# A squared-ReLU MLP on one core: w2 in two loads, x ahead of w1 on two queues, and x's tail columns transposed in pairs of row tiles

## The chip, the cores and the metric

The kernel runs on one core of a Trainium2 chip. The metric is device time in microseconds. Twelve runs of the kernel before gave a median of 291.34 us, from 290.75 to 291.82.

The names used below: PE is TensorE, DVE is VectorE, ACT is ScalarE, POOL is GpSimd, SP is SyncE. SP computes nothing here; it issues DMAs. ACT and POOL can issue DMAs too. Each engine has its own list of instructions, and instructions of different engines are ordered by semaphores.

## The reference

Input x is 2048 x 576, w1 is 576 x 4608, w2 is 4608 x 576, all bf16, with two bias vectors.

```python
def reference(x, w1, b1, w2, b2):
    h = jnp.einsum("bsd,df->bsf", x, w1) + b1
    zero = jnp.zeros_like(h)
    r = jnp.where(h > zero, h, zero)
    h = r * r
    out = jnp.einsum("bsf,fd->bsd", h, w2) + b2
    return out
```

## The kernel before

**Tiling.** The 2048 rows of x are worked in four blocks of 512. The 4608 columns of w1 make 36 tiles of 128 (`ft`). The first four of these (`G`) have weights of their own, `w1n` (four row tiles of 128 by 512 columns) and `w1n8` (the last 64 rows of w1). The other 32 are worked in pairs: their weights `w1_h` hold one tile of the pair on partitions 0 to 63 and the other on 64 to 127, so that two matmuls of 64 rows run side by side (lines 188 and 190). For that, x transposed (`xT`, named xTw in the profile) is kept in nine slots of 64 or 128 rows, some of them copied to the other half of the partitions: `dup_windows` (lines 117 to 120) makes two copies of 64 x 2048 elements on DVE.

**Stages.** `a_full` computes the first four tiles of h for a block, `a_rows` the other 32. `evac_h` takes each tile out of PSUM: ACT applies the bias and ReLU (line 176), DVE squares (line 177). `phase_t` computes the last 128 output columns transposed (line 270, bias `b2T` added by ACT at line 273), `phase_b` the other 448 (line 289, bias `b2_bc` added by DVE at line 291). The blocks go in two pairs: a of blocks 0 and 1, then t and b of both, then the same for blocks 2 and 3.

**The start.** The first block's x is loaded as four row tiles `xs` (x_sb) and transposed on TensorE with an identity; the transposes of the later blocks are made by DMA (`load_xT`, lines 122 to 127). While the first x is awaited, seven matmuls on constants run (line 63). For the first block `a_full` runs in the order "k_outer": `x_transpose` (line 149) of row tiles 0 and 1, ten transposes; `x_copies(0)` (lines 151 to 159), which moves them from PSUM to xT0 with DVE and ACT; then partial matmuls `part(h, k)` (line 227) over halves h of the block's rows and row tiles k of w1n, with the transposes of row tiles 2 and 3 between them; then the `pair` matmuls over w1n8 (lines 203 and 205). For the last 64 columns of x, each row tile has a fifth transpose, of its last 128 columns. `make_b1T` transposes b1's 36 rows of 128.

**Queues.** SP's list of loads is x 0, w1n 0, w1n 1, x 3, w1n 2, w1n 3, then w1_h in pairs of halves with w1n8 behind the first pair, load_xT(1), the last four w1_h, b2_bc, six w2 loads of six row tiles each, load_xT(2). ACT loads x 1 and x 2. POOL loads b1_rows and b2_col (the last 128 values of b2, one to a partition) and then casts b2_col to b2T (line 102).

`keep(...)` holds an instruction at its place in the program's order. The pools `ps_h` and `ps_o` hold four PSUM banks each, handed out in turn; a tile that gets a bank again waits until its former reader is done.

Of the kernel before, what the change touches and what calls it, by code (L numbers as in the profile page):

```python
# [11 lines left out]
BF16 = mybir.dt.bfloat16  # L12
FP32 = mybir.dt.float32
# [4 lines left out]
def kernel(  # L18
# [9 lines left out]
    nc = tc.nc  # L28
    keep = tc.keep_in_program_order
    P = 128  # L30
    H = 64
    x2 = x.flatten_outer_dims()
    out2 = out.flatten_outer_dims()
    S, D = x2.shape
    F = w1.shape[1]
    NFT = F // P
    NC = D // H
    NK = NC // 2
    G = 4
    GW = G * P  # L40
# [4 lines left out]
    RT = SB // P  # L45
    DT = P
    DM = D - DT

    const = ctx.enter_context(tc.tile_pool(name="const", bufs=1))
    wpool = ctx.enter_context(tc.tile_pool(name="wpool", bufs=1))  # L50
# [5 lines left out]
    ps_h = ctx.enter_context(tc.tile_pool(name="ps_h", bufs=4, space=PSUM))  # L56
    ps_o = ctx.enter_context(tc.tile_pool(name="ps_o", bufs=4, space=PSUM))

    wps = ps_o.tile([P, 512], FP32, name="wps", tag="po")
    ones = nc.const_aps.tensor(1.0, [P, 512], BF16)  # L60
    WARM = [512] * 6 + [128]
    for i, n in enumerate(WARM):
        keep(nc.tensor.matmul(wps[:, 0:n], lhsT=ones[:, 0:P], rhs=ones[:, 0:n], start=True, stop=True))  # L63

    xs = const.tile([P, RT, D], BF16, name="x_sb")
    w1n = wpool.tile([P, NK, GW], BF16, name="w1n")
    w1n8 = wpool.tile([P, G // 2, P], BF16, name="w1n8")
    w1_h = wpool.tile([P, NC, FH], BF16, name="w1_h")
    w1_v = w1.rearrange("(c p) f -> p c f", p=H)

    def load_x(eng, rt):
        keep(eng.dma_start(out=xs[:, rt, :], in_=x2[rt * P:(rt + 1) * P, :]))  # L72

    def load_w1n(eng, k):
        keep(eng.dma_start(out=w1n[:, k, :], in_=w1[k * P:(k + 1) * P, 0:GW]))  # L75

    def load_w1n8(eng, h):
        src = w1[NK * P:D, 0:GW].rearrange("p (i h f) -> p i h f", h=2, f=P)
        keep(eng.dma_start(out=w1n8[h * H:(h + 1) * H, :, :], in_=src[:, :, h, :]))

    def load_w1(eng, h, j0, j1):
        keep(eng.dma_start(out=w1_h[h * H:(h + 1) * H, :, j0 * P:j1 * P],
                      in_=w1_v[:, :, GW + h * FH + j0 * P:GW + h * FH + j1 * P]))

    load_x(nc.sync, 0)
    load_x(nc.scalar, 1)
    load_w1n(nc.sync, 0)
    load_x(nc.scalar, 2)
    load_w1n(nc.sync, 1)
    load_x(nc.sync, 3)  # L90
    for k in range(2, NK):
        load_w1n(nc.sync, k)

    ident = const.tile([P, P], BF16, name="ident")
    make_identity(nc, ident[:])
    b1_rows = const.tile([P, P], BF16, name="b1_rows")
    nc.gpsimd.memset(b1_rows[:], 0.0)
    nc.gpsimd.dma_start(out=b1_rows[0:NFT, :], in_=b1.rearrange("(ft p) -> ft p", p=P))
    b2_col = const.tile([P, 1], BF16, name="b2_col")
    nc.gpsimd.dma_start(out=b2_col[:], in_=b2[DM:D].rearrange("(d o) -> d o", o=1))  # L100
    b2T = const.tile([P, 1], FP32, name="b2T")
    nc.gpsimd.tensor_copy(out=b2T[:], in_=b2_col[:])
    warm = const.tile([P, 1], FP32, name="warm")
    keep(nc.scalar.activation(out=warm[:], in_=nc.const_aps.tensor(0.0, [P, 1], FP32), func=ACT.Relu))

    E3, O, SPC, E = 0, 1, 5, 6
    LO_W = [O, O + 1, O + 2, O + 3, E, E + 1, E + 2, E3, SPC]
# [9 lines left out]
    def dup_windows(sb):  # L117
        xT = xT_blk[sb]
        keep(nc.vector.tensor_copy(out=xT[0:H, SPC:SPC + 4, :], in_=xT[H:P, E3:E3 + 4, :]))  # L119
        keep(nc.vector.tensor_copy(out=xT[H:P, SPC:SPC + 4, :], in_=xT[0:H, O:O + 4, :]))  # L120
# [7 lines left out]

    w2_sb = wpool.tile([P, NFT, D], BF16, name="w2_sb")
    w2_view = w2.rearrange("(ft p) d -> p ft d", p=P)  # L130
    W2CH = 6

    def load_w2(c):
        keep(nc.sync.dma_start(out=w2_sb[:, c * W2CH:(c + 1) * W2CH, :], in_=w2_view[:, c * W2CH:(c + 1) * W2CH, :]))
# [3 lines left out]
    alloc_xT(0)  # L138
    xT0 = xT_blk[0]
    HS = SB // 2  # L140
    tb_po = [ps_o.tile([P, 2, HS], BF16, name="tb", tag="po") for _ in range(2)]
    tb_ph = [ps_h.tile([P, 2, HS], BF16, name="tb", tag="ph") for _ in range(4)]
    half_banks = [tb_ph, None]

    def x_transpose(j, k):
        h, q = divmod(j, 2)
        qc = slice(q * P, (q + 1) * P)
        bank, slot, c0 = (half_banks[h][k], 0, k * P) if k < NK else (half_banks[h][2], 1, D - P)
        keep(nc.tensor.transpose(bank[:, slot, qc], xs[:, j, c0:c0 + P], ident[:]))  # L149

    def x_copies(h):
        hc = slice(h * HS, (h + 1) * HS)
        for k in range(NK):
            src = half_banks[h][k][:, 0, :]
            if k % 2 == 0:
                keep(nc.vector.tensor_copy(out=xT0[:, O + k, hc], in_=src))  # L156
            else:
                keep(nc.scalar.copy(out=xT0[:, O + k, hc], in_=src))  # L158
        keep(nc.vector.tensor_copy(out=xT0[:, E3, hc], in_=half_banks[h][2][:, 1, :]))


    b1T = const.tile([P, NFT], FP32, name="b1T")

    def make_b1T():
        b1T_ps = ps_o.tile([P, P], BF16, name="b1T_ps", tag="po")
        keep(nc.tensor.transpose(b1T_ps[:], b1_rows[:], ident[:]))  # L166
        keep(nc.vector.tensor_copy(out=b1T[:], in_=b1T_ps[:, 0:NFT]))

# [26 lines left out]
    def a_full(sb, order):  # L195
        xT = xT_blk[sb]
        banks = []
        for g in range(G):
            pool, tag = (ps_o, "po") if g < 2 else (ps_h, "ph")
            banks.append(pool.tile([P, SB], FP32, name="pn", tag=tag))  # L200

        def pair(i, start, stop):
            keep(nc.tensor.matmul(banks[2 * i][:], lhsT=w1n8[0:H, i, :], rhs=xT[0:H, SPC, :],  # L203
                             start=start, stop=stop, skip_group_check=order == "k_outer"))
            keep(nc.tensor.matmul(banks[2 * i + 1][:], lhsT=w1n8[H:P, i, :], rhs=xT[H:P, E3, :],  # L205
                             start=start, stop=stop, skip_group_check=order == "k_outer"))

        def full(g, k, start, stop):
            keep(nc.tensor.matmul(banks[g][:], lhsT=w1n[:, k, g * P:(g + 1) * P], rhs=xT[:, O + k, :],  # L209
                             start=start, stop=stop))  # L210

        if order == "rows_first":
            for i in (1, 0):
                pair(i, True, False)
            for g in (2, 3, 0, 1):
                for k in range(NK):
                    full(g, k, False, k == NK - 1)
                evac_h(sb, banks[g], g)
        else:
            if order == "k_outer":  # L220
                tb_new = [ps_h.tile([P, 2, HS], BF16, name="tb", tag="ph") for _ in range(2)]
                half_banks[1] = tb_new + tb_po

                def part(h, k):
                    hc = slice(h * HS, (h + 1) * HS)
                    for g in range(G):
                        keep(nc.tensor.matmul(banks[g][:, hc], lhsT=w1n[:, k, g * P:(g + 1) * P],  # L227
                                              rhs=xT[:, O + k, hc], start=(h == 0 and k == 0), stop=False,
                                              skip_group_check=True))

                for j in range(2):
                    for k in range(NK):
                        x_transpose(j, k)
                for j in range(2):
                    x_transpose(j, NK)
                x_copies(0)
                part(0, 0)
                for k in range(NK + 1):
                    x_transpose(2, k)
                part(0, 1)  # L240
                part(0, 2)
                for k in range(NK + 1):
                    x_transpose(3, k)
                x_copies(1)
                dup_windows(0)
                part(0, 3)
                part(1, 0)
                make_b1T()
                for k in range(1, NK):
                    part(1, k)  # L250
            else:
                for g in (2, 3, 0, 1):
                    for k in range(NK):
                        full(g, k, k == 0, False)
            for i in (1, 0):
                pair(i, False, True)
                evac_h(sb, banks[2 * i], 2 * i)
                evac_h(sb, banks[2 * i + 1], 2 * i + 1)
# [35 lines left out]
    for (j0, j1) in [(0, 1), (1, 2), (2, 4), (4, 6), (6, 8), (8, 10), (10, 12)]:  # L294
        load_w1(nc.sync, 0, j0, j1)
        load_w1(nc.sync, 1, j0, j1)
        if j0 == 0:
            load_w1n8(nc.sync, 0)
            load_w1n8(nc.sync, 1)
    load_xT(1)  # L300
    for (j0, j1) in [(12, 14), (14, 16)]:
        load_w1(nc.sync, 0, j0, j1)
        load_w1(nc.sync, 1, j0, j1)
    keep(nc.sync.dma_start(out=b2_bc[:], in_=b2.partition_broadcast(P)))
    for c in (0, 3, 1, 4, 2, 5):
        load_w2(c)
    load_xT(2)

# [51 lines left out]
```

## Time and profile before

One execution was taken by the hardware profiler. Beside the lines shown in the prediction, these are the values to have at hand:

| what | value |
|---|---|
| median of 12 runs | 291.34 us |
| profiled execution, own time | 291.82 us |
| its span, first to last instruction | 290.1 us |
| granted TensorE clock | 1.0 |
| first x transpose on PE starts | 3.39 us |
| PE idle from 6.36 to 6.95 us, for a w1n transfer | 0.59 us |
| first pair of `a_rows` on PE starts | 10.45 us |
| first read of w2 on PE starts | 76.6 us |
| last w2 load issued, and its time to landing | 36.65 us, 10.5 us |

A time that the text calls a start is counted from the start of the span. A line of the timeline gives start, duration, engine with source line, operation, the tile written and the tile read, and how often. In brackets stands how long the engine was idle before, and what ended that. An engine's name with a q (SPq) is its instruction queue, issuing DMAs. Busy shares of different engines overlap, so they do not add up to the span.

### The profile page before, as it was taken

How to read it: one execution, taken by the hardware profiler on the slowest of the kernel's cores; microseconds unless marked ns; L12 is line 12 of the kernel's file. 1: busy time of each engine (PE TensorE's matmuls, PEld its weight loads, DVE VectorE, ACT ScalarE, POOL GpSimd, SP SyncE). 2: the span in 40 equal slices, each digit the busy share in tenths (PEclk: the TensorE clock that was granted, in tenths of full speed). 3: DMA queues.
4: the chain of work that ended last, by engine and by line, in shares of the span. 5: the costliest groups of instructions: out<-in, count | busy, mean ns of one | idle time of the engine just before them, and what ended most of it. 6: DMA issues, size and time to landing. Idle time of an engine off the chain costs nothing.

```text
span 290.1 us, 4699 instructions
## 1 busy us (share of the span) xinstructions
PE 285.7 (98%) x2032; PEld 139.7 (48%) x2032; DVE 78.5 (27%) x176; ACT 96.6 (33%) x154; POOL 2.2 (1%) x10
## 2 busy tenths in 40 slices
PE   8999999999999999999999999999999999999995
PEld 4644444444444555555544444444444455555554
DVE  1644554444500200000015444444440001100001
ACT  2566666666500000000027666666670000000000
POOL 3000000000000000000000000000000000000000
DMA  7999999300001200000000000000000110000000
GB/s 200 215 244 192 313 390 220 76 0 2 0 13 26 52 16 18 16 16 18 16 16 2 1 2 0 2 0 2 0 2 0 36 38 16 16 17 30 21 16 18
DMA packets 31637, 16.52 MB, mean 57 GB/s; under 512 B 15732, under 2 KB 31616, under 8 KB 31616
## 3 DMA queue, kind: packets, MB, share of 16 engines
q1 hardware_dynamic: 31264, 15.91, 21.9%
q8 instruction: 16, 0.26, 0.4%
q10 hardware_dynamic: 288, 0.30, 0.3%
q14 instruction: 5, 0.04, 0.0%
q0 software_dynamic: 64, 0.01, 0.0%
HBM read 11.36 MB, written 2.36 MB: 47 GB/s over the span
## 4 chain that ended last, share of the span: by engine, by line
PE 97%; DMA 1%; SPq 1%; issue 0%; DVE 0%
PE ph L188 42%; PE po L289 38%; PE pt L270 11%; PE pn L209 4%; DMA w1n<-in_w_dram 1%; PE pn L227 1%; PE ph L190 1%; PE pn L203 1%; SPq L75 0%; SPq L72 0%; DVE o_sb L291 0%; PE tb L149 0%; PE b1T_ps L166 0%; PE pn L205 0%
## 5 line engine op out<-in xcount | busy, mean ns | idle before, releaser
L188 PE MATMUL ph<-xTw,w_h 64*128 64x512 bf16 x576 | 124.6, 376 | 0.0
L190 PE MATMUL ph<-xTw,w_h 64*128 64x512 bf16 x576 | 124.6, 376 | 0.0
L289 PE MATMUL po<-w_sb,hT 128*128 128x448 bf16 (+2 forms) x612 | 109.4, 341 | 0.0
L176 ACT ACTIVATE r<-ph,b1T 128x512 bf16<-128x512 f32 x128 | 81.0, 684 | 41.7 <-PE ph L190 41.7
L188 PEld LDWEIGHTS <-w_h 64*128 64x128 bf16 x576 | 54.1, 94 | 68.3
L289 PEld LDWEIGHTS <-hT 128*128 128x128 bf16 x612 | 58.5, 98 | 51.0
L177 DVE TENSOR_TENSOR hT<-r 128x512 bf16<-128x512 bf16 x144 | 61.1, 425 | 75.9 <-ACT r L176 75.4
L190 PEld LDWEIGHTS <-w_h 64*128 64x128 bf16 x576 | 54.1, 94 | 0.0
L291 DVE TENSOR_TENSOR o_sb<-po,b_bc 128x448 bf16<-128x448 f32 (+2 forms) x17 | 10.1, 597 | 125.8 <-PE po L289 125.8
L270 PE MATMUL pt<-hT,w_sb 128*128 128x512 bf16 x144 | 31.4, 379 | 0.0
L176 ACT ACTIVATE r<-pn,b1T 128x512 bf16<-128x512 f32 x16 | 10.3, 687 | 61.0 <-PE pn L205 59.6
L270 PEld LDWEIGHTS <-w_sb 128*128 128x128 bf16 x144 | 14.1, 98 | 17.0
L273 ACT ACTIVATE oT<-pt,b2T 128x512 bf16<-128x512 f32 x4 | 2.7, 687 | 28.3 <-PE pt L270 28.3
L209 PE MATMUL pn<-xTw,w1n 128*128 128x512 bf16 x48 | 10.9, 379 | 0.0
L209 PEld LDWEIGHTS <-w1n 128*128 128x128 bf16 x48 | 4.5, 98 | 6.0 <-issue 0.8
L227 PE MATMUL pn<-xTw,w1n 128*128 128x256 bf16 x32 | 4.6, 289 | 0.6 <-DMA w1n<-in_w_dram 0.6
L227 PEld LDWEIGHTS <-w1n 128*128 128x128 bf16 x32 | 3.1, 103 | 1.2 <-DMA w1n<-in_w_dram 0.9
L63 PE MATMUL wps<-const-bfloat16-1.0 128*128 128x512 bf16 (+1 forms) x7 | 2.8, 578 | 0.8 <-PEq L344 0.8
L156 DVE COPY xTw<-tb 128x256 bf16<-128x256 bf16 x4 | 1.1, 292 | 6.9 <-PE tb L149 6.9
L119 DVE COPY xTw<-xTw 64x2048 bf16<-64x2048 bf16 x4 | 2.8, 690 | 0.2
L120 DVE COPY xTw<-xTw 64x2048 bf16<-64x2048 bf16 x4 | 2.8, 688 | 0.1
L158 ACT COPY xTw<-tb 128x256 bf16<-128x256 bf16 x4 | 1.3, 375 | 3.9 <-PE tb L149 3.9
(23 smaller groups left out, 16.2 us busy)
## 6 DMA issues: line engine op xcount, KB each, us to landing
w_sb<-in_w_dram SPq DMA_DIRECT2D x6, 864.0 KB, 9.8
w_h<-in_w_dram SPq DMA_DIRECT2D x14, 288.0 KB, 6.4
out_dram<-o_sb SPq DMA_DIRECT2D x15, 112.0 KB, 1.7
w_h<-in_w_dram SPq DMA_DIRECT2D x4, 144.0 KB, 3.4
w1n<-in_w_dram SPq DMA_DIRECT2D x4, 128.0 KB, 4.0
out_dram<-ot SPq DMA_DIRECT2D x4, 128.0 KB, 2.0
x_sb<-in_x_dram ACTq DMA_DIRECT2D x2, 144.0 KB, 3.0
x_sb<-in_x_dram SPq DMA_DIRECT2D x2, 144.0 KB, 3.2
```

Of the source, the lines that this page charges most:

```text
L63: keep(nc.tensor.matmul(wps[:, 0:n], lhsT=ones[:, 0:P], rhs=ones[:, 0:n], start=True, stop=True))
L119: keep(nc.vector.tensor_copy(out=xT[0:H, SPC:SPC + 4, :], in_=xT[H:P, E3:E3 + 4, :]))
L176: keep(nc.scalar.activation(out=r[:], in_=bank[:], func=ACT.Relu, bias=b1T[:, ft:ft + 1], scale=1.0))
L177: keep(nc.vector.tensor_tensor(out=hTs[sb][:, ft, :], in0=r[:], in1=r[:], op=ALU.mult))
L188: keep(nc.tensor.matmul(bx[:], lhsT=w1_h[0:H, LO_C[i], jc], rhs=xT[0:H, LO_W[i], :], start=(i == 0), stop=(i == NC - 1)))
L190: keep(nc.tensor.matmul(by[:], lhsT=w1_h[H:P, UP_C[i], jc], rhs=xT[H:P, UP_W[i], :], start=(i == 0), stop=(i == NC - 1)))
L203: keep(nc.tensor.matmul(banks[2 * i][:], lhsT=w1n8[0:H, i, :], rhs=xT[0:H, SPC, :], start=start, stop=stop, skip_group_check=order == "k_o ...
L209: keep(nc.tensor.matmul(banks[g][:], lhsT=w1n[:, k, g * P:(g + 1) * P], rhs=xT[:, O + k, :], start=start, stop=stop))
L227: keep(nc.tensor.matmul(banks[g][:, hc], lhsT=w1n[:, k, g * P:(g + 1) * P], rhs=xT[:, O + k, hc], start=(h == 0 and k == 0), stop=False, s ...
L270: keep(nc.tensor.matmul(pt[:], lhsT=w2_sb[:, ft, DM:D], rhs=hT[:, ft, :], start=(i == 0), stop=(i == NFT - 1)))
L289: keep(nc.tensor.matmul(po[:, 0:d1 - d0], lhsT=hT[:, ft, jj * P:(jj + 1) * P], rhs=w2_sb[:, ft, d0:d1], start=(i == 0), stop=(i == NFT - 1)))
L291: keep(nc.vector.tensor_tensor(out=o_sb[:, d0:d1], in0=po[:, 0:d1 - d0], in1=b2_bc[:, d0:d1], op=ALU.add))
```

## The change

- x comes first: row tiles 0 and 2 on SP, 1 and 3 on ACT. The four w1n loads follow, alternately on SP and ACT. The two w1n8 loads, now each of all 512 columns, and the b1 load are issued by ACT, after its table load. The zeroing of b1_rows goes from POOL to DVE.
- b2_col is loaded by SP, after the last w1_h load and before b2_bc. The cast to b2T stays on POOL; in the program it now stands behind the w1_h loads and before the call of `a_full`.
- w2 is loaded in two transfers of 18 row tiles each instead of six of six.
- `x_transpose(j)` makes the four full transposes of a row tile. The 64 tail columns of two row tiles are put side by side in `xs8` by a copy on POOL and transposed together, so there are 16 + 2 = 18 transposes instead of 20. DVE copies the result to two slots of xT0, and three more copies on DVE fill the duplicate slots, in place of `dup_windows(0)`.
- All transposes and copies of the first block now stand before the first `part`.
- The line 63 matmuls write to a bank of ps_h instead of ps_o, and the last has 256 columns instead of 128; the four banks of the first `a_full` all come from ps_o, the transposes and b1T_ps from ps_h.

```diff
-    wps = ps_o.tile([P, 512], FP32, name="wps", tag="po")
+    wps = ps_h.tile([P, 512], FP32, name="wps", tag="ph")
-    WARM = [512] * 6 + [128]
+    WARM = [512] * 6 + [256]
...
+    b1_rows = const.tile([P, P], BF16, name="b1_rows")
+    nc.vector.memset(b1_rows[:], 0.0)
     load_x(nc.sync, 0)
     load_x(nc.scalar, 1)
-    load_w1n(nc.sync, 0)
-    load_x(nc.scalar, 2)
-    load_w1n(nc.sync, 1)
-    load_x(nc.sync, 3)
-    for k in range(2, NK):
-        load_w1n(nc.sync, k)
+    load_x(nc.sync, 2)
+    load_x(nc.scalar, 3)
+    for k in range(NK):
+        load_w1n(nc.sync if k % 2 == 0 else nc.scalar, k, k + 1)
 
     ident = const.tile([P, P], BF16, name="ident")
     make_identity(nc, ident[:])
-    b1_rows = const.tile([P, P], BF16, name="b1_rows")
-    nc.gpsimd.memset(b1_rows[:], 0.0)
-    nc.gpsimd.dma_start(out=b1_rows[0:NFT, :], in_=b1.rearrange("(ft p) -> ft p", p=P))
-    b2_col = const.tile([P, 1], BF16, name="b2_col")
-    nc.gpsimd.dma_start(out=b2_col[:], in_=b2[DM:D].rearrange("(d o) -> d o", o=1))
-    b2T = const.tile([P, 1], FP32, name="b2T")
-    nc.gpsimd.tensor_copy(out=b2T[:], in_=b2_col[:])
     warm = const.tile([P, 1], FP32, name="warm")
     keep(nc.scalar.activation(out=warm[:], in_=nc.const_aps.tensor(0.0, [P, 1], FP32), func=ACT.Relu))
+    for h in range(2):
+        load_w1n8(nc.scalar, h)
+    keep(nc.scalar.dma_start(out=b1_rows[0:NFT, :], in_=b1.rearrange("(ft p) -> ft p", p=P)))
...
-    W2CH = 6
+    W2CH = 18
...
+    def x_transpose(j):
         h, q = divmod(j, 2)
-        qc = slice(q * P, (q + 1) * P)
-        bank, slot, c0 = (half_banks[h][k], 0, k * P) if k < NK else (half_banks[h][2], 1, D - P)
-        keep(nc.tensor.transpose(bank[:, slot, qc], xs[:, j, c0:c0 + P], ident[:]))
+        for k in range(NK):
+            bank, slot = PLACE[k]
+            keep(nc.tensor.transpose(tb[h][bank][:, slot, q * P:(q + 1) * P], xs[:, j, k * P:(k + 1) * P], ident[:]))
+
+    def x_transpose_tail(h):
+        keep(nc.gpsimd.tensor_copy(out=xs8[:, 2 * h:2 * h + 2, :], in_=xs[:, 2 * h:2 * h + 2, NK * P:D]))
+        keep(nc.tensor.transpose(tb[1][0][:, 2, h * P:(h + 1) * P], xs8[:, 2 * h:2 * h + 2, :], ident[:]))
+
+    def x_copies_tail():
+        src = tb[1][0][:, 2, :].rearrange("p (h t) -> p h t", h=2)
+        for q in range(2):
+            keep(nc.vector.tensor_copy(out=xT0_q[H:P, E3, :, q, :], in_=src[q * H:(q + 1) * H, :, :]))
+        for q in range(2):
+            keep(nc.vector.tensor_copy(out=xT0_q[0:H, SPC, :, q, :], in_=src[q * H:(q + 1) * H, :, :]))
+        keep(nc.vector.tensor_copy(out=xT0[0:H, E:E + 3, :], in_=xT0[H:P, O:O + 3, :]))
+        keep(nc.vector.tensor_copy(out=xT0[0:H, E3, :], in_=xT0[H:P, O + 3, :]))
+        keep(nc.vector.tensor_copy(out=xT0[H:P, SPC:SPC + 4, :], in_=xT0[0:H, O:O + 4, :]))
 
     def x_copies(h):
         hc = slice(h * HS, (h + 1) * HS)
-        for k in range(NK):
-            src = half_banks[h][k][:, 0, :]
-            if k % 2 == 0:
-                keep(nc.vector.tensor_copy(out=xT0[:, O + k, hc], in_=src))
-            else:
-                keep(nc.scalar.copy(out=xT0[:, O + k, hc], in_=src))
-        keep(nc.vector.tensor_copy(out=xT0[:, E3, hc], in_=half_banks[h][2][:, 1, :]))
+        for k in (0, 1):
+            keep(nc.vector.tensor_copy(out=xT0[:, O + k, hc], in_=tb[h][0][:, k, :]))
+        keep(nc.scalar.copy(out=xT0[:, O + 2:O + 4, hc], in_=tb[h][1][:, 0:2, :]))
...
                 for j in range(2):
-                    for k in range(NK):
-                        x_transpose(j, k)
-                for j in range(2):
-                    x_transpose(j, NK)
+                    x_transpose(j)
                 x_copies(0)
-                part(0, 0)
-                for k in range(NK + 1):
-                    x_transpose(2, k)
-                part(0, 1)
-                part(0, 2)
-                for k in range(NK + 1):
-                    x_transpose(3, k)
+                for j in range(2, RT):
+                    x_transpose(j)
                 x_copies(1)
-                dup_windows(0)
-                part(0, 3)
+                for h in range(2):
+                    x_transpose_tail(h)
+                x_copies_tail()
+                for k in range(NK):
+                    part(0, k)
                 part(1, 0)
                 make_b1T()
...
         load_w1(nc.sync, 1, j0, j1)
-        if j0 == 0:
-            load_w1n8(nc.sync, 0)
-            load_w1n8(nc.sync, 1)
     load_xT(1)
     for (j0, j1) in [(12, 14), (14, 16)]:
         load_w1(nc.sync, 0, j0, j1)
         load_w1(nc.sync, 1, j0, j1)
+    b2_col = const.tile([P, 1], BF16, name="b2_col")
+    keep(nc.sync.dma_start(out=b2_col[:], in_=b2[DM:D].rearrange("(d o) -> d o", o=1)))
+    b2T = const.tile([P, 1], FP32, name="b2T")
+    nc.gpsimd.tensor_copy(out=b2T[:], in_=b2_col[:])
     keep(nc.sync.dma_start(out=b2_bc[:], in_=b2.partition_broadcast(P)))
-    for c in (0, 3, 1, 4, 2, 5):
+    for c in range(2):
         load_w2(c)
     load_xT(2)
```

More of the change, by code (lines that the diff above doesn't have):

```diff
@@ L66 @@
     w1n = wpool.tile([P, NK, GW], BF16, name="w1n")
-    w1n8 = wpool.tile([P, G // 2, P], BF16, name="w1n8")
+    w1n8 = wpool.tile([P, GW], BF16, name="w1n8")
     w1_h = wpool.tile([P, NC, FH], BF16, name="w1_h")
@@ L72, in load_x, with load_w1n @@
         keep(eng.dma_start(out=xs[:, rt, :], in_=x2[rt * P:(rt + 1) * P, :]))
-    def load_w1n(eng, k):
-        keep(eng.dma_start(out=w1n[:, k, :], in_=w1[k * P:(k + 1) * P, 0:GW]))
+    def load_w1n(eng, k0, k1):
+        src = w1[k0 * P:k1 * P, 0:GW].rearrange("(k p) f -> p k f", p=P)
+        keep(eng.dma_start(out=w1n[:, k0:k1, :], in_=src))
     def load_w1n8(eng, h):
-        src = w1[NK * P:D, 0:GW].rearrange("p (i h f) -> p i h f", h=2, f=P)
-        keep(eng.dma_start(out=w1n8[h * H:(h + 1) * H, :, :], in_=src[:, :, h, :]))
+        keep(eng.dma_start(out=w1n8[h * H:(h + 1) * H, :], in_=w1[NK * P:D, 0:GW]))
     def load_w1(eng, h, j0, j1):
@@ L140 @@
     HS = SB // 2
[L141 to L145, printed above, removed]
-        h, q = divmod(j, 2)
-        qc = slice(q * P, (q + 1) * P)
-        bank, slot, c0 = (half_banks[h][k], 0, k * P) if k < NK else (half_banks[h][2], 1, D - P)
-        keep(nc.tensor.transpose(bank[:, slot, qc], xs[:, j, c0:c0 + P], ident[:]))
+    tb = [[ps_h.tile([P, 4, HS], BF16, name="tb", tag="ph") for _ in range(2)] for _ in range(2)]
@@ new lines @@
+    PLACE = [(0, 0), (0, 1), (1, 0), (1, 1)]
+    xs8 = const.tile([P, RT, H], BF16, name="xs8")
+    xT0_q = xT0.rearrange("p c (h q t) -> p c h q t", h=2, q=2)
+    def x_transpose(j):
+        h, q = divmod(j, 2)
+        for k in range(NK):
[4 more added lines that the diff above has]
+        keep(nc.tensor.transpose(tb[1][0][:, 2, h * P:(h + 1) * P], xs8[:, 2 * h:2 * h + 2, :], ident[:]))
@@ L162 @@
+        keep(nc.scalar.copy(out=xT0[:, O + 2:O + 4, hc], in_=tb[h][1][:, 0:2, :]))
     b1T = const.tile([P, NFT], FP32, name="b1T")
     def make_b1T():
-        b1T_ps = ps_o.tile([P, P], BF16, name="b1T_ps", tag="po")
+        b1T_ps = ps_h.tile([P, P], BF16, name="b1T_ps", tag="ph")
         keep(nc.tensor.transpose(b1T_ps[:], b1_rows[:], ident[:]))
@@ L198, in a_full @@
         for g in range(G):
-            pool, tag = (ps_o, "po") if g < 2 else (ps_h, "ph")
+            pool, tag = (ps_o, "po") if g < 2 or order == "k_outer" else (ps_h, "ph")
             banks.append(pool.tile([P, SB], FP32, name="pn", tag=tag))
         def pair(i, start, stop):
-            keep(nc.tensor.matmul(banks[2 * i][:], lhsT=w1n8[0:H, i, :], rhs=xT[0:H, SPC, :],
+            keep(nc.tensor.matmul(banks[2 * i][:], lhsT=w1n8[0:H, 2 * i * P:(2 * i + 1) * P], rhs=xT[0:H, SPC, :],
                              start=start, stop=stop, skip_group_check=order == "k_outer"))
-            keep(nc.tensor.matmul(banks[2 * i + 1][:], lhsT=w1n8[H:P, i, :], rhs=xT[H:P, E3, :],
+            keep(nc.tensor.matmul(banks[2 * i + 1][:], lhsT=w1n8[H:P, (2 * i + 1) * P:(2 * i + 2) * P], rhs=xT[H:P, E3, :],
                              start=start, stop=stop, skip_group_check=order == "k_outer"))
@@ L220, in a_full @@
             if order == "k_outer":
-                tb_new = [ps_h.tile([P, 2, HS], BF16, name="tb", tag="ph") for _ in range(2)]
-                half_banks[1] = tb_new + tb_po
                 def part(h, k):
```

## The prediction

> **What bounds the kernel now.** I read the page's busy shares first, then the chain that ended last, then the timelines of PE, SP and POOL over the first 35 us, since the diff touches little beyond the start.
>
> ```profile
> PE 285.7 (98%) x2032; PEld 139.7 (48%) x2032; DVE 78.5 (27%) x176; ACT 96.6 (33%) x154; POOL 2.2 (1%) x10
> ...
> PE ph L188 42%; PE po L289 38%; PE pt L270 11%; PE pn L209 4%; DMA w1n<-in_w_dram 1%; PE pn L227 1%; PE ph L190 1%; PE pn L203 1%; SPq L75 0%; SPq L72 0%; DVE o_sb L291 0%; PE tb L149 0%; PE b1T_ps L166 0%; PE pn L205 0%
> ```
>
> TensorE is busy for 98% of the span and carries 97% of the chain. So there is almost nothing to win: before the end, only the DMA pieces of 1% are not matmuls. The other side is that TensorE has no slack behind which a new wait could disappear. A wait put in front of the first matmuls moves everything after it.
>
> The PE timeline at the start (start, duration, instruction; in brackets the idle time and what ended it):
>
> ```profile
> 0.78 2.82 PE L63 MATMUL wps<-const-bfloat16-1.0 128*128 128x512 bf16 x7 [0.78 <-PEq L344]
> ...
> 3.39 1.27 PE L149 MATMUL tb<-ident,x_sb 128*128 128x128 bf16 x10
> ...
> 6.95 0.61 PE L227 MATMUL pn<-xTw,w1n 128*128 128x256 bf16 x4 [0.59 <-DMA w1n<-in_w_dram]
> ...
> 8.60 1.47 PE L227 MATMUL pn<-xTw,w1n 128*128 128x256 bf16 x12
> 10.01 0.39 PE L203 MATMUL pn<-xTw,w1n 64*128 64x512 bf16 x1
> ```
>
> The first pair over w1's last 64 rows starts at 10.01; this is my reference point, because after it both programs issue the same matmuls in the same order. Before it the one stall of note is 0.59 us (with 0.87 on the weight loads) for a w1n transfer.
>
> Then SP's and POOL's own timelines:
>
> ```profile
> 6.36 12.04 SPq L82 DMA_DIRECT2D w_h<-in_w_dram  x12
> 18.45 4.60 SPq L126 DMA_TRANSPOSE xTw<-in_x_dram  x1
> 23.10 1.25 SPq L127 DMA_TRANSPOSE xTw<-in_x_dram  x1
> 24.39 2.65 SPq L82 DMA_DIRECT2D w_h<-in_w_dram  x4
> 27.09 0.67 SPq L304 DMA_DIRECT2D b_bc<-in_b_dram  x1
> ...
> 2.12 0.56 POOL L100 DMA_DIRECT2D b_col<-in_b_dram  x1
> 5.89 0.18 POOL L102 CAST b2T<-b_col 128x1 f32<-128x1 bf16 x1 [3.21 <-DMA b_col<-in_b_dram]
> ```
>
> SP issues all of w1 and two transposes before it reaches b2_bc at 27.09. POOL waits 3.21 us for b2_col and then casts it. Today this harms nobody, since nothing stands behind the cast on POOL. Last, what the DMA view (size and time from issue to landing) says of issues near 26 to 27 us:
>
> ```profile
> w_h<-in_w_dram SPq DMA_DIRECT2D x2, 288.0 KB, 6.7
> ...
> b_bc<-in_b_dram SPq DMA_DIRECT2D x1, 144.0 KB, 6.4
> ```
>
> **What the Trainium skill says.** "TensorE: Matmul & The Clock Gate", table at the head of the page: the queues of ScalarE, VectorE and GpSimdE are strict FIFO. No run here shows it for POOL yet (its cast is last), but the step below rests on it. The same page, Part 1: after an idle window of about 3.4 us the array falls back to half rate, and about 3.4 us of sustained work restore it. The trace agrees with a slow start: the 512-column weight loads of L63 start 0.43 us apart, the matmuls of L188 0.215 us apart. L227's matmuls take 417 ns at most and 273 in the median. "DMA: Bandwidth & Descriptors", Queues, rings and completion order: each engine consumes a ring's descriptors in order; here b2_bc, issued at 27.09, lands at 33.5, behind w1's last 288 KB (about 26.4 plus 6.7, 33.1).
>
> **The change part by part.**
>
> *b2_col and the cast (the term that decides).* The load moves from POOL's queue at 2.12 to SP's, behind all of w1 and load_xT(1), at the place of b2_bc. The cast of b2T stays on POOL, and in the program it stands before a_full, so before the two new copies into xs8. The compiled order of the changed kernel confirms it:
>
> ```
> POOL  L302 TensorCopy b2T<-b_col 128x1      [waits the b2_col DMA]
> POOL  L149 TensorCopy xs_121<-x_sb 128x128  [waits x 0, x 1]
> POOL  L149 TensorCopy xs_121<-x_sb 128x128  [waits x 2, x 3]
> PE    L150 Ldweights xs_121                 [waits POOL]
> PE    L230 Ldweights w1n                    (the first of the 32 partial matmuls)
> ```
>
> So the tail transposes, and behind them on PE every matmul of w1n, wait for a DMA of 256 bytes at the end of SP's list. When does it land? SP's early list loses two w1n (0.90 us) and two w1n8 issues (1.30) to ACT, but in the compiled order each later issue waits for the DMA eight places earlier, so SP starts w1 at about 3.6 as now (x 1 was issued at 0.73 and lands 2.8 later). By my walk through these waits the first 288 KB go out near 6.5 instead of 7.7, 1.2 us sooner. From 10 us on the DMA share of the windows is near or over 1.0, so the lead can only be kept. Landing L is then 33.1 - 1.2 plus some 0.2 for its own descriptors: 32.1 us. Bounds: 30 (lead of the full 2.2 us, landing 5 after issue at 25) and 33.5 (no lead, landing where b2_bc does).
>
> After L: cast 0.18 plus 0.07 to wake (5.89 against 2.12 + 3.7 for the landing). Two POOL copies of 128x128 are not in the trace; nearest are POOL's MEMSET of that size at 0.20 us and the select at 0.28. I take 0.25 each; bounds 0.2 and 1.0, since POOL spans are rough. The second tail transpose ends near L + 1.0, of which the first matmul waits. Then 32 partial matmuls and b1T's transpose: at full rate 0.113 each (13 in 1.47 us), 3.7 us. TensorE has by then been idle from about 6 us to 32, so it restarts slow: between 0.78 and 5.76 it needed 4 to 5 us to come up. With 4.4 us at 0.213 apiece (half of 0.43) 20.6 matmuls pass, the remaining 12.4 take 1.4: 5.8 us. Bounds 3.7 (no slow phase) and 7.0 (all slow). DVE's seven tail copies lie beside this: four near 0.28 (as L159), one near 0.52 and one near 0.2 (L119's 0.69 scaled by size), and one of 0.69, 2.5 us, done at about L + 3.6, before the pair needs them at L + 6.7. If that cover went, the rest of 2.5 us would show.
>
> The pair starts at L + 1.0 + 5.8 = 38.9 instead of 10.01: +28.9; I round down the overlap of wake and weight load by 0.3 and take **+28.6 us**. By bounds: 30 + 0.8 + 3.7 - 10 = +24.5 to 33.5 + 2.0 + 7.0 - 10 = +32.5.
>
> *Is any of it regained?* After 10 us TensorE waits for no DMA today, so the data that arrive during the stall buy nothing. The rest shifts as a block. load_xT(3) waits for the first block's matmuls and shifts with them.
>
> *x on two queues, w1n alternating, w1n8 and b1 on ACT.* They could remove the stall of 0.59 to 0.87 us; all w1n has landed by 7 us, so under the wait it is worth nothing. On ACT the w1n8 and b1 loads now wait for x 0, x 2 and w1n 1, and behind them stand ACT's two copies out of PSUM; the last of these waits ends when w1n 1 lands, by about 6 us, so the copies end near 7.5, long before L. With no stall at L they would delay part(0, 2) by 1 to 2 us. b1's zeroing moves from POOL (0.20 us) to an idle DVE.
>
> *20 transposes become 18; six copies out of PSUM instead of ten, plus tail.* Two matmuls fewer: about 0.2 us, before L, hidden. All transposes now precede the partial matmuls, so nothing fills PE while it waits; that is why the stall is whole.
>
> *w2 in fewer transfers.* The short description says four of nine; the code has W2CH = 18 and range(2), so two of eighteen. Six take 27.81 to about 47 now (36.65 + 10.5), first read by L270 at 76.6; afterwards that read is near 105. Two transfers of 2.6 MB at the same rate land near 48: nothing. Even landing 25 us late they would be hidden.
>
> *Warm-up of 256 instead of 128 columns, PSUM pools swapped.* +0.1 us in front of x's landing, hidden.
>
> **Sum.** The profiled execution took 291.82 (span 290.1): 291.8 + 28.6 = 320.4. The median of the runs is 0.48 below it: 319.9.
>
> **Rivals.**
> 1. *The wait as above, 316.9 to 322.9*: chance 0.84. For it: the compiled order, the SP timeline, PE at 98%.
> 2. *A short wait:* the 256 bytes land 3.7 us after issue at 25 as they did from POOL's queue: L = 28.7, +25.2, 316.5 or, with no slow restart, 314.4. Against it: b2_bc needed 6.4 in that place. Chance 0.07.
> 3. *The other side, no wait:* if POOL takes the copies ahead of the cast, or b2_col passes the w1 queue and lands before about 5.5 us, the point from which it decides. Then x 3 is there at 4.5 (1.2 + 3.3), eight transposes at 0.127 end at 5.5, the tail at 6.0, 33 matmuls at 0.113 at 9.7: -0.3 us, 291.0, with 0.7 either way. Chance 0.05, of which 0.02 is over 0.2% faster.
> 4. *A longer wait:* POOL copies of 1 us and more, or b2_col held until the 2.6 MB transfers behind it have passed: L near 36, about 324. Chance 0.04.
>
> **How the numbers follow.** The forecast is 320. Range 317 to 323: the first rival, which leaves out about 0.16. About 0.2% (0.6 us) is what this kernel's measurement can tell from none. Slower 0.95, same 0.03, faster 0.02.
>
> **What would show it.** In the changed profile: POOL's cast idle some 26 us for b_col and starting near 32; L150's weight loads waiting for POOL; PE slices 1 to 4 nearly empty; L230's matmuls at 400 ns or so at first; L209's first at about 38.6; w_sb landed before 50. Wrong would be a cast that starts before 10, or a pn matmul of L230 ahead of it.

## The result: 319.14 us, slower by 9.6%

The changed kernel took 319.14 us in the median of 8 runs (318.62 to 320.27); the kernel before, run beside it, 291.36 (32 runs). The ratio is 1.0959, with a 95% interval of 1.0946 to 1.0971. The profiled execution took 318.82 us with a span of 316.9, so 27.0 us more than the one before by its own time and 26.8 by its span.

The page of the changed kernel: busy shares, then the rows of the 40 slices for PE, its clock and the DMA engines, then the chain that ended last.

```profile
PE 287.3 (91%) x2030; PEld 140.4 (44%) x2030; DVE 79.3 (25%) x180; ACT 96.3 (30%) x152; POOL 1.4 (0%) x9
...
PE   5000999999999999999999999999999999999996
...
PEclk9555799999999999999999999999999999999999
DMA  7999990012000011000000000000000012000001
...
PE ph L194 39%; PE po L287 34%; PE pt L268 10%; PE pn L215 3%; PE pn L230 2%; PE ph L196 1%; PE pn L209 1%; PE tb L150 0%; POOL xs L149 0%; POOL ident masks.py:199 0%; DVE o_sb L289 0%; POOL ident masks.py:197 0%; POOL b2T L302 0%; PE b1T_ps L172 0%; POOLq masks.py:199 0%
```

TensorE was busy for nearly the same time, 287.3 us against 285.7. Its slices 2 to 4 are empty, and those are the slices in which the DMA engines bring in w1. The clock that it was granted is 0.5 in the same slices and about 0.7 in the fifth, where its work begins again. (The row shows nothing of the slow matmuls at the very start, in slice 1.) The chain does not name the culprit: 9% of the span (29.61 us) stands there as "issue", time for which it found no releaser. The view of waits names it (engine and line, what it waited for, total, times, longest):

```profile
POOL b2T L302 <- DMA b_col<-in_b_dram: 29.6, 1, 29.6
...
PEld L150 <- POOL xs L149: 26.4, 1, 26.4
DVE xTw L155 <- PE tb L150: 26.4, 1, 26.4
PE tb L150 <- POOL xs L149: 26.2, 1, 26.2
```

One wait of POOL, one of PE on POOL, one of DVE on PE: a single stall passed on. The timelines give its place. From SP, POOL and PE, in this order:

```profile
3.64 12.86 SPq L82 DMA_DIRECT2D w_h<-in_w_dram  x14
16.54 5.22 SPq L122 DMA_TRANSPOSE xTw<-in_x_dram  x1
...
25.79 0.83 SPq L300 DMA_DIRECT2D b_col<-in_b_dram  x1
...
30.93 0.19 POOL L302 CAST b2T<-b_col 128x1 f32<-128x1 bf16 x1 [29.63 <-DMA b_col<-in_b_dram]
31.05 0.53 POOL L149 COPY xs<-x_sb 128x128 bf16<-128x128 bf16 x2
...
3.50 1.68 PE L146 MATMUL tb<-ident,x_sb 128*128 128x128 bf16 x16
31.40 0.52 PE L150 MATMUL tb<-ident,xs 128*128 128x128 bf16 x2 [26.23 <-POOL xs L149]
31.72 4.21 PE L230 MATMUL pn<-xTw,w1n 128*128 128x256 bf16 x20
35.76 0.22 PE L172 MATMUL b1T_ps<-ident,b_rows 128*128 128x128 bf16 x1
35.82 1.47 PE L230 MATMUL pn<-xTw,w1n 128*128 128x256 bf16 x12
37.22 0.39 PE L209 MATMUL pn<-xTw,w1n 64*128 64x512 bf16 x1
```

The data that the two copies on POOL need, x, were there before 5 us: in the first run below the same copies start at 3.73 and 4.57. Here they ran at 31.05, right behind a cast that nobody needs before phase_t. Twenty partial matmuls then took 4.21 us, 0.21 each; the next twelve, behind b1's transpose, took 1.47. The reference point, the first pair over w1's last 64 rows, moved from 10.01 to 37.22, by 27.2 us. From there the two kernels run in step: the last addition of a bias on DVE starts 277.07 us after the pair in both. The span is shorter by 0.4 us behind that, in the last store and the end of the program.

### The profile page after: what moved, and what is told of

The parts are those of the page before. It is cut to its first block, busy times and chain, and to the rows that moved or that the text cites. A ratio compares the mean times of both kernels' runs of the same rounds, so it can differ in the third digit from the quotient of the medians.

```text
span 316.9 us, 4698 instructions
## 1 busy us (share of the span) xinstructions
PE 287.3 (91%) x2030; PEld 140.4 (44%) x2030; DVE 79.3 (25%) x180; ACT 96.3 (30%) x152; POOL 1.4 (0%) x9
## 4 chain that ended last, share of the span: by engine, by line
PE 89%; issue 9%; POOL 0%; DVE 0%; POOLq 0%
PE ph L194 39%; PE po L287 34%; PE pt L268 10%; PE pn L215 3%; PE pn L230 2%; PE ph L196 1%; PE pn L209 1%; PE tb L150 0%; POOL xs L149 0%; POOL ident masks.py:199 0%; DVE o_sb L289 0%; POOL ident masks.py:197 0%; POOL b2T L302 0%; PE b1T_ps L172 0%; POOLq masks.py:199 0%
## 5 line engine op out<-in xcount | busy, mean ns | idle before, releaser
L215 PEld LDWEIGHTS <-w1n 128*128 128x128 bf16 x48 | 4.5, 98 | 6.0 <-issue 0.8
L230 PE MATMUL pn<-xTw,w1n 128*128 128x256 bf16 x32 | 5.6, 354 | 0.0
L230 PEld LDWEIGHTS <-w1n 128*128 128x128 bf16 x32 | 4.0, 128 | 1.2
L211 PE MATMUL pn<-xTw,w1n 64*128 64x512 bf16 x8 | 2.4, 379 | 0.0
```

## Experiments

### The cast out of the way, and the load out of the way

First the cast alone is moved, behind the call of the first a_full; b2_col is still loaded late.

```diff
-    nc.gpsimd.tensor_copy(out=b2T[:], in_=b2_col[:])
...
     a_full(0, "k_outer")
+    nc.gpsimd.tensor_copy(out=b2T[:], in_=b2_col[:])
```

> The changed kernel with only the cast of b2T moved behind the first a_full on POOL's list, so that the two copies into xs8 no longer stand behind it; the load of b2_col stays late on SP. Theory (POOL's list order is the whole loss): the 27.8 us go, and what is left is the new start itself. From the changed kernel's trace I work it out: transposes done at 5.2, ACT's copies at 6.6 to 7.7 because its b1 load waits in front of them, 25 matmuls of 0.113 from 7.1, and b1's rows landing near 9 with 12 matmuls still to come, so the pair over the last 64 rows near 10.5 instead of 10.01: 291.9 us (290.8 to 292.6). Rival (the late b2_col or the new order of loads costs by itself, not POOL's list): above 300. Rival (the new start is a gain once the wait is gone): 290.6 or less.

Measured: 291.84 us (22 runs), ratio to before 1.0018 (1.0012 to 1.0025). POOL's and PE's timelines of this run:

```profile
4.57 0.29 POOL L149 COPY xs<-x_sb 128x128 bf16<-128x128 bf16 x1 [0.54 <-DMA x_sb<-in_x_dram]
32.34 0.19 POOL L309 CAST b2T<-b_col 128x1 f32<-128x1 bf16 x1 [27.48 <-DMA b_col<-in_b_dram]
...
7.28 1.47 PE L230 MATMUL pn<-xTw,w1n 128*128 128x256 bf16 x12 [0.31 <-ACT xTw L166]
...
9.03 0.23 PE L172 MATMUL b1T_ps<-ident,b_rows 128*128 128x128 bf16 x1 [0.28 <-DMA b_rows<-in_b_dram]
...
10.50 0.39 PE L209 MATMUL pn<-xTw,w1n 64*128 64x512 bf16 x1
```

The reader is to see that POOL waits for b2_col nearly as long as in the changed kernel (27.48 us against 29.63) and that it costs nothing, because nothing is behind it. Moving one instruction took back 27.3 us. Against the kernel before 0.5 us are left. In this execution the pair comes at 10.50 instead of 10.01, with the two small waits shown. But these are single executions, and the one of the kernel before is the slowest of its twelve. In the third run below, which has the same loads, the pair comes at 9.99 and the median is the same. That the new start costs the 0.5 us is likely; which wait it is made of is not shown.

Second, the cast stays in front and its data come early (the line that allocates b2_col moves along):

```diff
+    nc.gpsimd.dma_start(out=b2_col[:], in_=b2[DM:D].rearrange("(d o) -> d o", o=1))
     warm = const.tile([P, 1], FP32, name="warm")
...
-    keep(nc.sync.dma_start(out=b2_col[:], in_=b2[DM:D].rearrange("(d o) -> d o", o=1)))
```

> The changed kernel with b2_col loaded by POOL near its start, as in the kernel before, and the cast still in front of the xs8 copies. Theory: the cast's wait then ends near 5 us (issue near 1.3 plus 3.7), the tail transposes come at about 5.6, and the time is that of the run with the cast moved, up to 0.4 us more: 292 us. Rival (a cast ahead of the copies on POOL is itself what costs, whenever its data land): 300 or more.

Measured: 292.20 us (17 runs), ratio 1.0032 (1.0020 to 1.0044). POOL's timeline:

```profile
5.32 0.19 POOL L302 CAST b2T<-b_col 128x1 f32<-128x1 bf16 x1 [3.00 <-DMA b_col<-in_b_dram]
5.45 0.53 POOL L151 COPY xs<-x_sb 128x128 bf16<-128x128 bf16 x2
```

The execution that these lines are from took 294.71 us, the slowest of the 17 (the next took 292.65), so only its order and the landing near 5 us are read from it. So it is the product of the two edits that costs, a late load and an instruction order that puts the copies behind it. Undoing either one is enough.

Third, the same wait on POOL, but the copies on DVE:

```diff
-        keep(nc.gpsimd.tensor_copy(out=xs8[:, 2 * h:2 * h + 2, :], in_=xs[:, 2 * h:2 * h + 2, NK * P:D]))
+        keep(nc.vector.tensor_copy(out=xs8[:, 2 * h:2 * h + 2, :], in_=xs[:, 2 * h:2 * h + 2, NK * P:D]))
```

> The changed kernel with the two copies into xs8 done by DVE instead of POOL; POOL's cast still waits for the late b2_col. Theory (the loss is who stands behind the cast, not the wait itself): POOL still waits until about 31 us and nobody follows; the tail transposes start 0.3 to 0.6 us later than in the run with the cast moved, since DVE does the copies after its own four: 292.2 us (291.4 to 293). Rival (POOL's wait holds up something else as well): above 300.

Measured: 291.83 us, ratio 1.0020 (1.0012 to 1.0028). From PE and POOL:

```profile
5.84 0.33 PE L150 MATMUL tb<-ident,xs 128*128 128x128 bf16 x2 [0.57 <-DVE xs L149]
...
9.99 0.39 PE L209 MATMUL pn<-xTw,w1n 64*128 64x512 bf16 x1
...
31.63 0.19 POOL L302 CAST b2T<-b_col 128x1 f32<-128x1 bf16 x1 [30.33 <-DMA b_col<-in_b_dram]
```

POOL's cast runs at 31.63 and nobody waits for it. DVE's copies cost even less than expected, as the tail transposes start at 5.84, where they were with POOL (5.82).

### Two parts of the change in the kernel before

The late b2_col with its cast, put into the kernel before, where POOL has nothing behind it:

> The kernel before with only the load of b2_col moved to SP behind w1, and its cast behind it, as in the changed kernel; POOL has nothing behind the cast here. Theory: POOL's cast waits until about 31 us and nobody notices: 291.4, within 0.2%. Rival (the late load costs wherever it stands): 10 us or more slower.

Measured: 291.28 us, ratio 0.9995 (0.9985 to 1.0005); the cast waits until 33.00. The w2 loads alone (W2CH = 18, range(2)):

> The kernel before with only the w2 loads changed, two of 18 row tiles instead of six of six. Theory: hidden, since w2 is first read at 76.6 us and lands by 50: 291.4, within 0.2%. Rival (two big transfers hold up load_xT(2) or later loads): slower by 0.5 us or more.

Measured: 291.08 us, ratio 0.9992 (0.9985 to 1.0000): at most 0.4 us faster, and not told from none. Neither costs anything by itself in the kernel before.

### The dose

b2_col and the cast go up SP's list, in front of the fifth of the seven pairs of w1_h loads. (The lines at their old place go, and both tiles are allocated ahead of the loop; this is not shown.)

```diff
     for (j0, j1) in [(0, 1), (1, 2), (2, 4), (4, 6), (6, 8), (8, 10), (10, 12)]:
+        if j0 == 6:
+            keep(nc.sync.dma_start(out=b2_col[:], in_=b2[DM:D].rearrange("(d o) -> d o", o=1)))
+            nc.gpsimd.tensor_copy(out=b2T[:], in_=b2_col[:])
         load_w1(nc.sync, 0, j0, j1)
...
```

> The changed kernel with the load of b2_col and its cast moved up SP's list, in front of the fifth of the seven pairs of w1_h loads that stand ahead of load_xT(1); the cast is still in front of the xs8 copies. Theory: the time follows the landing of b2_col one for one. In the changed kernel that place of SP's list is reached at 9.9 us and loads issued there take about 6 us, so b2_col lands near 15.7 instead of 30.9, and the time is 319.1 - 15.2 = 303.9 us (302.5 to 305.3); the idle stretch is still long enough for the slow restart. Rival (a loss that doesn't depend on the landing): 315 to 320.

Measured: 303.70 us (4 runs, 302.86 to 304.53), ratio 1.0423 (1.0400 to 1.0446). SP, POOL and PE of this run:

```profile
10.12 1.13 SPq L296 DMA_DIRECT2D b_col<-in_b_dram  x1
...
15.85 0.19 POOL L297 CAST b2T<-b_col 128x1 f32<-128x1 bf16 x1 [14.55 <-DMA b_col<-in_b_dram]
...
16.64 4.47 PE L230 MATMUL pn<-xTw,w1n 128*128 128x256 bf16 x20
...
21.01 1.98 PE L230 MATMUL pn<-xTw,w1n 128*128 128x256 bf16 x12
22.92 0.39 PE L209 MATMUL pn<-xTw,w1n 64*128 64x512 bf16 x1
```

In this execution the cast came 15.1 us earlier than in the changed kernel's, and the pair and the execution's own time 14.3 us earlier. The missing 0.8 us lies between cast and pair, 7.07 us against 6.29: the slow matmuls went on into the next twelve, which took 1.98 us instead of 1.47. So the loss follows the landing to within 1 us, and the slow phase behind it is not always of the same length. The medians differ by 15.4 us, but this one is of four runs, with granted clocks from 0.976 to 1.000; that it fell so near to the 303.9 expected is in part luck.

### The slow restart

Matmuls on constants fill TensorE's wait; their bank is cleared by the first real matmul, and the rest is as in the changed kernel.

```diff
+                for _ in range(215):
+                    keep(nc.tensor.matmul(banks[3][:, 0:HS], lhsT=ones[:, 0:P], rhs=ones[:, 0:HS],
+                                          start=True, stop=True, skip_group_check=True))
                 for h in range(2):
                     x_transpose_tail(h)
```

> The changed kernel with 215 matmuls on constants (256 columns, into a PSUM bank that the first real matmul clears) between the full transposes and the tail transposes, so that TensorE works during the wait: about 24 us of work that ends near 29.5, before b2_col lands. Theory (the restart at half rate is 20 matmuls of 0.21 us instead of 0.113, 1.95 us): 319.1 - 2.0 = 317.1 us (316.4 to 317.8). Rival (the restart costs nothing on the path, because DVE's tail copies would hold the pair matmuls anyway): 319.

Measured: 321.67 us (4 runs, 319.65 to 322.43), so slower than the changed kernel by 2.5 us where 2.0 less was expected. In its profile the filler ends at 29.1, b2_col's cast starts only at 32.75, 1.8 later than in the changed kernel, PE still idles before the tail transposes, and the first 20 matmuls are slow:

```profile
33.23 0.52 PE L150 MATMUL tb<-ident,xs 128*128 128x128 bf16 x2 [4.13 <-POOL xs L149]
...
33.55 4.47 PE L230 MATMUL pn<-xTw,w1n 128*128 128x256 bf16 x20
```

The filler was too short for its purpose, and the landing moved. What the run does show is that 4.13 us of idling bring the slow matmuls back. What they cost it does not show, so it was repeated with 240:

> As the run with matmuls on constants during the wait, with 240 instead of 215 of them, 27.1 us of work that ends near 31.9, so that TensorE's idle stretch before the tail transposes is about 1.5 us instead of 4.1. Read from the profile, as the time also moves with the landing of b2_col (30.9 in the changed kernel, 32.7 with 215 matmuls): the stretch from the start of POOL's cast to the pair over the last 64 rows was 6.29 us in the changed kernel. Theory (restart at half rate costs about 1.95 us): 4.3 us, with the first 20 matmuls of L230 in about 2.4 us instead of 4.2 to 4.5. Rival (it isn't the idle stretch that makes these slow): 6.2 us or more. Time by the theory 317.2 us plus whatever the landing is later than 30.9.

Measured: 319.18 us (4 runs, 318.06 to 319.63). POOL and PE:

```profile
33.60 0.19 POOL L305 CAST b2T<-b_col 128x1 f32<-128x1 bf16 x1 [32.30 <-DMA b_col<-in_b_dram]
...
34.08 0.47 PE L150 MATMUL tb<-ident,xs 128*128 128x128 bf16 x2 [1.35 <-POOL xs L149]
34.38 2.35 PE L230 MATMUL pn<-xTw,w1n 128*128 128x256 bf16 x20
...
38.02 0.39 PE L209 MATMUL pn<-xTw,w1n 64*128 64x512 bf16 x1
```

With only 1.35 us of idling the 20 matmuls took 2.35 us instead of 4.21, and cast to pair took 4.42 us instead of 6.29. The mean clock granted in this execution was 1.000, against 0.957 in the changed kernel's. The restart is worth 1.87 us in this pair of executions. The total did not fall, because b2_col's cast came 2.7 us later (33.60 against 30.93), which took the gain back: later by 2.67, shorter by 1.87, and the execution's own time was 0.81 us longer (319.63 against 318.82).

### Is the new start worth anything without the stall?

On top of the moved cast, b1's load goes to POOL:

```diff
+    nc.gpsimd.dma_start(out=b1_rows[0:NFT, :], in_=b1.rearrange("(ft p) -> ft p", p=P))
     warm = const.tile([P, 1], FP32, name="warm")
...
-    keep(nc.scalar.dma_start(out=b1_rows[0:NFT, :], in_=b1.rearrange("(ft p) -> ft p", p=P)))
```

> The run with the cast moved, and in addition b1's load issued by POOL near its start instead of by ACT. Theory: ACT's two copies out of PSUM no longer stand behind a DMA issue that waits for w1n 1 (2.5 us of waiting before them), and b1's transpose no longer waits for its rows: PE's gaps of 0.31 before part(0, 2) and 0.28 before b1's transpose go, 291.84 - 0.6 = 291.2 us. Rival (the gaps are the w1n transfers, not ACT's list): 291.8.

Then the tail transposes go ahead of the second half's copies:

```diff
-                x_copies(1)
                 for h in range(2):
                     x_transpose_tail(h)
+                x_copies(1)
```

> As the run with b1 on POOL, with the two tail transposes moved in front of the second half's copies, so that they wait for POOL alone and not for DVE (PE stood 0.37 us there in the run with the cast moved). Theory: another 0.3 us, 290.9 us, slightly under the kernel before. Rival (PE then waits for DVE at part(0, 0) or for w1n instead): 291.2.

Measured: 291.60 us, ratio 1.0011 (1.0003 to 1.0019), and 291.68, ratio 1.0012 (1.0003 to 1.0022). They missed by 0.4 and 0.8 us. In the first the two gaps are gone from the profile, but PE now waits 0.29 us for w1n before the first partial matmuls. Its median lies between the theory's 291.2 and the rival's 291.8, and it is not told from that of the run with the cast moved: the ratios to the kernel before, 1.0011 and 1.0018, have intervals that overlap. In the second PE no longer waits for DVE, but the PE line of the first partial matmuls says what is late next (this execution took 292.33 us, the slowest of its 14):

```profile
6.83 2.52 PE L230 MATMUL pn<-xTw,w1n 128*128 128x256 bf16 x20 [1.51 <-DMA w1n<-in_w_dram]
```

The w1n transfers took 5.4 to 5.7 us to land in this execution and 4.9 to 5.1 with b1 on POOL alone, against 3.8 to 4.4 in the run with the cast moved. They stand behind x in all three, and go out at the same times, from 1.7 us on; so the order alone does not explain it. What differs is b1's load, which POOL issues near 1.4 us, where ACT issued it near 6. The other profiles of the new start fit this: with b2_col loaded by POOL at 1.25 us, w1n took 4.9 to 5.5 us, and in the six profiles in which POOL issues no load, 3.5 to 4.6. So b1's load on POOL may have cost what it saved; each figure is one execution, and no run tests it. No version of the new start is clearly faster than the kernel before.

## Why the prediction was right, step by step

- **The cast in front of the copies**: as predicted. The runs with the cast moved, with b2_col early and with the copies on DVE each take the whole stall away, by three ways. That POOL works its list strictly in order, for which the prediction had only "TensorE: Matmul & The Clock Gate" of the Trainium skill (table at the head), is what this trace shows too: copies whose data came before 5 us ran at 31.05, behind the waiting cast.
- **Landing at 32.1**: too late by 1.2 us, the largest miss of the sum. From issue to landing b2_col took 5.1 us, where my sum implied some 6.2, carried over from w1's last loads and b2_bc; that is between the sum and the 3.7 of the rival with a short wait. It did land right behind w1's last load (near 30.7), as the sum had it, but that load was quicker: 5.6 us instead of 6.7. The lead of SP came out at 1.3 us (b2_col issued at 25.79, against b2_bc at 27.09), predicted 1.2, but this is luck. The first load of 288 KB, from which the 1.2 was taken, went out at 7.19, not near 6.5: a lead of 0.5 us. At load_xT(1) the lead was 1.9 us (16.54 against 18.45), so it was not just kept. And in the other runs with this list of loads on SP, b2_col went out anywhere from 25.75 to 28.48.
- **The copies, the transposes and the 33 matmuls**: predicted at 6.5 us from landing to pair after rounding, measured 6.29 from cast to pair. POOL's two copies took 0.53 us together, near the 0.5 taken, and 20 matmuls ran at about half rate, where I had 20.6. Part 1 of "TensorE: Matmul & The Clock Gate" in the Trainium skill puts both the idling that slows TensorE and the work that brings it back at about 3.4 us. The idling fits: 4.13 and 26.23 us slowed it, 1.35 did not. The slow phase was longer here, from 31.40 to about 35.7, 4.3 us, and the measurement decides; the prediction's 4.4 came from the trace of before. The run with the longer filler prices the restart at 1.87 us. It was 0.8 us more in the run of the dose, so the agreement to the tenth here is in part luck.
- **DVE's tail copies hidden**: yes. They ended at 34.66, 2.6 us before the pair.
- **w2, the two queues, two transposes fewer**: nothing, as said. For w2 the run of that part alone shows it; here w2 had landed by about 46 us. For the other two it is read from the trace only: all of it lies before the wait.
- **Nothing regained later**: as said, up to the last addition of a bias, which moved by 27.2 us like the pair. The span moved by 26.8.
- **The rival on the other side**: it never came to pass, but the run with the cast moved tests its number. It gave 291.0, with 0.7 either way, for the start without the wait; measured 291.84, just outside. It left out ACT, whose two copies stand behind three DMA issues, and b1's rows, which land near 9. The prediction named the first of these and did not put it into that sum. They are not the whole miss: with both gone, in the run with b1 on POOL, the time was still 291.60, 0.6 above the 291.0, with a wait for w1n that the sum had not foreseen either.

The forecast for the profiled execution was 320.4 and it took 318.82; of the 1.6 us, 1.2 are the landing and the rest the small terms.

## What to carry to other kernels

Before an engine that only did chores is given work on the critical path, read its whole list: the new work inherits every wait in front of it, and a load of 256 bytes is as late as the queue that it stands in (its cast ran at 5.3, 15.9 or 30.9 us here, by its place). The cast was not held in place, and in every run it ran where the program text had it, so a harmless cast must be written below the urgent work. When the chain of waits shows a long "issue", look in the view of waits for the engine that waited just as long.

## What was not expected of the hardware

The same list of loads on SP does not always land alike. b2_col's cast started at 30.9 us in the changed kernel, where TensorE was idle, and at 31.6 (copies on DVE), 32.3 (cast moved), 32.8 and 33.6 (the two fillers), 33.3 (b1 on POOL) and 34.9 (tail transposes first), where it worked. That a busy TensorE delays the loads would fit, and all six are later. But 31.6 is close to 30.9, the last two also have the early load of POOL, and each figure is one execution: the changed kernel's own runs spread over 1.6 us. It stays open.
